# Row sums of two attention blocks in one product, spread over the partitions by transfers, and the first keys turned in parts of 512 and 256 tokens

## The chip, the cores and the metric

The kernel runs on one core of a Trainium2 chip. The core has a matrix engine (TensorE, PE in the profile), three engines for elementwise work (VectorE or DVE, ScalarE or ACT, GpSimd or POOL) and a SyncE queue (SP) that issues most transfers. The metric is the device time of one execution in microseconds; lower is better. Time before: 901.92 us, the median of 3 runs (901.76 to 902.88).

## What is computed

A routed attention and then a two-layer network with an ELU between its layers. Batch 4, 8 heads, 768 tokens, head size 64, 16 clusters; then 3072 tokens of width 512 through a hidden layer of 2048.

```python
q_assign = argmax(einsum(q_n, c_n));  k_assign = argmax(einsum(k_n, c_n))
mask = q_assign[:, :, :, None] == k_assign[:, :, None, :]
scores = where(mask, scale * q @ k.T, -1e9)
attn = exp(scores - max);  attn = attn / (sum(attn) + 1e-9)
x = (attn @ v) as rows of 512            # tokens x (heads * head size)
h = x @ w_in
g = where(h > 0, h, exp(min(h, 0)) - 1)
out = g @ w_out
```

## The kernel before

**Stages.** All data but the cluster masks (bf16) is float32. A first stage computes attention (about 18 to 341 us of the profile), then come six groups of 512 tokens of the network (341 us to the end), whose products are split after Strassen's manner into seven. The order of all instructions is written out by hand: each engine works through its own instructions in the order in which the program issues them, and semaphores hold an instruction until its operands are ready and its destination is free.

**Blocks and slots.** Attention is cut into 32 blocks (`blocks`, L156): batch, half of the queries (384 tokens) and pair of heads. `slot(n)` (L632) holds, one beside the other, the scores of block n, the product with V of block n-1, and the division of block n-2. Keys and queries lie turned (head size on partitions, tokens along the row) in `kT` and `qT`; the keys of batches 0 and 2 borrow the last 768 columns of `xT`, the array that later holds the attention's result.

In one slot the engines do this, in this order:
- PE: `row_sums(n-2)` (L552): for each head of the pair a product of 64 columns of ones with the summed probabilities of that head, into the bank `d_bank`, so that each of 64 rows holds the row sums. Then `values(n-1)` (L533) into `o_bank`; in some slots `clusters_q` or `clusters_k` (L427), four products of 32 columns each into `d_bank`, which give the similarity to the cluster centres; then six times `plain` (L498) and `masked` (L511), which put scores of 128 keys into one of three double banks in turn (`ring`).
- ACT: `take_sums(n-2)` (L563 to L565): logarithm of the row sums, a copy of them, and the exponential of minus the logarithm, an approximate reciprocal, into `r_of` and `e_of`. Then `take_values(n-1)` (L550), six exponentials (L520), and at the end what the list `later` holds (`flush`, L396): copies of the cluster masks (L456) and the exponent step of a weight piece (L330).
- DVE: `sums_end` (L528, L529): sums of the probabilities of block n-1 into `summed`; `divide(n-2)` (L568, L569): one Newton step on the reciprocal; in cluster slots `assign` (L440 to L453: transpose, maximum, comparison, transpose); the transposes of the next batch's keys and queries (L659, L666 to L673); `weigh(n)` (L401), which fills the rest of the slot with pieces of the weights' conversion (L320 to L350: the input's float64 words are joined into float32); and, behind the fourth exponential, `sums_begin` (L523).
- POOL: the multiplication of the result by the reciprocal (L572), and `mask_q` (L463), flushed after the cluster copies.
- SP: loads of V for block n+1 (L182), of raw keys and queries (L166) and of weights (L300).

How much of the weights' conversion goes into a slot is fixed by a table written by hand, `ROOM` (L384), against costs in `COST` (L389). The change does not touch either.

**The start.** `slot_first` (L596) turns queries and keys by products with the identity (`turned`, L588), 384 tokens at a time, in ring order, finds the clusters of both halves of the keys, and runs the scores of block 0. `masked(0, kt)` needs the cluster masks of the keys' half that kt lies in.

**The end of attention.** After the last slot come the rows' sums of block 30 and the values of block 31 (L1397 to L1405). `finish_attention` (L1407) runs inside the network's first unit, between its second and third product. In the first group POOL also forms sums of weights (`w_step`, L719) and stores them by its own transfers (L732), and bounds the ELU's exponentials (L762).

The lines that hold a division step and the multiplication:

```python
nc.vector.tensor_tensor(e_of, e_of, r_of, op=Alu.mult)
nc.vector.scalar_tensor_tensor(
    r_of, e_of, -2.0, r_of, op0=Alu.add, op1=Alu.mult, accum_out=r_sum[:, n : n + 1]
)
nc.gpsimd.tensor_tensor(x_of(n), x_of(n), r_of, op=Alu.mult)
```

Of the kernel before, what the change touches and what calls it, by code (L numbers as in the profile page):

```python
# [61 lines left out]
def main_path(ctx, tc, c, q, k, v, centroids, moe_w_in, moe_w_out, out):  # L62
# [71 lines left out]
    top = early[:, 7488:7512]  # L134
    hot_q = early[:, 7512:7896].bitcast(BF16).rearrange("p (s n) -> p s n", s=2)
# [3 lines left out]
    summed = sums_w[:, 4 * HS : 6 * HS]  # L139
# [111 lines left out]
    cT = const.tile([P, P], F32, name="cT")  # L251
    count = const.tile([P, 4 * B], F32, name="count")
    counted = 0
    r_sum = const.tile([P, len(blocks)], F32, name="r_sum")
    d_sum = const.tile([P, len(blocks)], F32, name="d_sum")
# [54 lines left out]
    def begin():  # L310
# [19 lines left out]
        later.append(lambda: nc.scalar.activation(e, e, Act.Relu, scale=8.0, bias=off))  # L330
# [63 lines left out]
    credit, later = 0.0, []  # L394

    def flush():  # L396
        for other in later:
            other()
        later.clear()
# [25 lines left out]
    def similar(t, cols, ps):  # L425
        for pr in range(NPR):
            nc.tensor.matmul(  # L427
                ps[32 * pr : 32 * pr + 32, :HS],
                lhsT=cT[:, 32 * pr : 32 * pr + 32],
                rhs=t[pr][:, cols],  # L430
                start=True,
                stop=True,
            )

    def assign(hot, ps):
# [3 lines left out]
        n = HS // NC  # L439
        nc.vector.transpose(sim, ps[:, :HS])  # L440
# [31 lines left out]
    def clusters_k(b, half, ps):  # L472
        cols = ts(half, HS)
# [13 lines left out]
    turn_of = 0  # L487
# [39 lines left out]
    def sums_end():  # L527
        nc.vector.tensor_tensor(add_to, add_to, probs_all[:, 8 * HS :], op=Alu.add)  # L528
        nc.vector.tensor_tensor(  # L529
            summed, add_to[:, : 2 * HS], add_to[:, 2 * HS :], op=Alu.add  # L530
# [21 lines left out]
    def row_sums(n):  # L552
        for e in range(2):
            nc.tensor.matmul(  # L554
                d_bank[64 * e : 64 * e + 64, :HS],
                lhsT=ones,
                rhs=summed[:, ts(e, HS)],
# [4 lines left out]
    def take_sums(n):  # L562
        nc.scalar.activation(r_of, d_bank[:, :HS], Act.Ln)  # L563
        nc.scalar.activation(e_of, d_bank[:, :HS], Act.Copy, accum_out=d_sum[:, n : n + 1])
        nc.scalar.activation(r_of, r_of, Act.Exp, scale=-1.0)  # L565

    def divide(n):
        nc.vector.tensor_tensor(e_of, e_of, r_of, op=Alu.mult)  # L568
        nc.vector.scalar_tensor_tensor(  # L569
            r_of, e_of, -2.0, r_of, op0=Alu.add, op1=Alu.mult, accum_out=r_sum[:, n : n + 1]  # L570
        )
        nc.gpsimd.tensor_tensor(x_of(n), x_of(n), r_of, op=Alu.mult)  # L572
# [8 lines left out]
    def turn(to, t, n):  # L581

        for i in range(HT):
            turned_by_pe(to[:, ts(i, P)], t, n + i)

    turns = 0

    def turned(to, t, n):  # L588
# [4 lines left out]
        turn(bank, t, n)  # L593
        nc.scalar.copy(to, bank[:, :HS])

    def slot_first():  # L596
# [10 lines left out]
        for pr in range(NPR):  # L607
            turned(kT[0][pr][:, :HS], first_k[pr], 0)
        told = [clusters_k(0, 0, o_bank)]
        flush()  # L610
        for pr in range(NPR):
# [1104 lines left out]
```

## Time and profile before

| | |
|---|---|
| Median of the runs | 901.92 us |
| The profiled execution | 902.24 us, of which its span is 900.5 us |
| PE busy | 889.9 us (99%) |
| DVE busy | 725.9 us (81%) |
| ACT busy | 449.5 us (50%) |
| POOL busy | 226.0 us (25%) |
| Granted PE clock, mean | 0.999 |

The page of a profile gives each engine's busy time, a strip of 40 equal slices of the span with the busy share of each in tenths, the transfers, the chain of work that ended last (followed back from the last instruction to what released it), and groups of instructions by line. A group's line reads: line, engine, operation, destination and source, shapes, count, busy time, mean duration. Closer views list single instructions in order of time with what ended the engine's idle time before each, the waits between engines, and the busy time of each engine in chosen stretches.

The two strips that matter here, where each digit is a slice of about 22.5 us:

```
PE   8999999999999999999999999999999999999997
DVE  4699999999999997995389965895589558956885
```

### The profile page before, as it was taken

What the parts mean: (1) busy time and instruction counts of PE and PEld (TensorE: products, weight loads), DVE (VectorE), ACT (ScalarE), POOL (GpSimd) and SP (SyncE); (2) the same over time, 40 slices, a digit from 0 to 9 for tenths busy, and PEclk for the clock granted to TensorE, in tenths of its full rate; (3) what the DMA queues carried; (4) which work ended last, traced back from release to release, by engine and by line L of the source; (5) the groups of instructions that cost most, each with busy time, mean ns of one, the idle gap of its engine ahead of it and who ended that gap; (6) DMA issues with size and microseconds to landing.
All of it is one profiled execution on the core that took longest, in us unless ns stands there. A gap on an engine that the chain in (4) does not pass through costs nothing.

```text
span 900.5 us, 17050 instructions
## 1 busy us (share of the span) xinstructions
PE 889.9 (99%) x6473; PEld 687.6 (76%) x6473; DVE 725.9 (81%) x1067; ACT 449.5 (50%) x883; POOL 226.0 (25%) x257
## 2 busy tenths in 40 slices
PE   8999999999999999999999999999999999999997
PEld 4444444444444447899989999999999999999997
DVE  4699999999999997995389965895589558956885
ACT  5677787777776774420133225522552255225421
POOL 1022031221303244870033002520252025202300
PEclk9999999999999999999999999999999999999999
DMA  6765554365323622102698766176717761767272
GB/s 197 195 110 137 153 137 80 105 135 139 71 82 96 192 88 71 70 13 95 199 296 302 241 206 220 50 242 206 218 55 241 212 210 58 240 210 209 58 221 87
DMA packets 153209, 138.33 MB, mean 154 GB/s; under 512 B 89248, under 2 KB 106656, under 8 KB 152096
## 3 DMA queue, kind: packets, MB, share of 16 engines
q1 hardware_dynamic: 151584, 132.45, 50.2%
q0 software_dynamic: 1248, 4.20, 1.5%
q8 instruction: 53, 0.87, 0.4%
q10 hardware_dynamic: 288, 0.52, 0.2%
q14 instruction: 36, 0.29, 0.1%
HBM read 114.59 MB, written 21.50 MB: 151 GB/s over the span
## 4 chain that ended last, share of the span: by engine, by line
PE 92%; DVE 4%; DMA 2%; SPq 1%; issue 0%; ACT 0%; DVEq 0%
PE bank L994 23%; PE bank L748 16%; PE banks L498 12%; PE o_bank L536 12%; PE bank L1066 9%; PE o_bank L994 4%; PE o_bank L748 3%; PE banks L511 3%; PE d_bank L994 2%; PE d_bank L554 2%; PE o_bank L1066 2%; PE d_bank L427 1%; SPq L166 1%; DMA w_out<-in_k_dram 1%; PE d_bank L1066 1%; PE d_bank L748 1%
## 5 line engine op out<-in xcount | busy, mean ns | idle before, releaser
L520 ACT ACTIVATE p_out<-banks 128x768 f32<-128x768 f32 x192 | 155.2, 811 | 26.8 <-PE banks L511 25.4
L536 PE MATMUL o_bank<-p_out,kq_g 128*64 128x384 f32 x768 | 129.4, 486 | 0.1
L536 PEld LDWEIGHTS o_bank<-p_out,kq_g 128*64 128x64 f32 x768 | 55.0, 137 | 69.2 <-issue 62.7
L762 POOL TENSOR_SCALAR kq_g<-kq_g 128x512 f32<-128x512 f32 x96 | 67.8, 715 | 152.0 <-ACT kq_g L761 151.6
L572 POOL TENSOR_TENSOR xT<-xT,sums_w 128x384 f32<-128x384 f32 x32 | 35.3, 1103 | 222.0 <-DVE sums_w L569 164.6
L523 DVE TENSOR_TENSOR sums_w<-p_out 128x1536 f32<-128x1536 f32 x32 | 57.1, 1785 | 7.5 <-ACT p_out L520 7.5
L994 PE MATMUL bank<-w_out,kq_g 128*128 128x128 f32 x512 | 63.1, 275 | 0.0
L528 DVE TENSOR_TENSOR sums_w<-sums_w,p_out 128x1536 f32<-128x1536 f32 x32 | 59.0, 1845 | 3.3 <-DVE sums_w L523 0.5
L994 PEld LDWEIGHTS bank<-w_out,kq_g 128*128 128x128 f32 x512 | 60.5, 192 | 0.5
L761 ACT ACTIVATE kq_g<-bank 128x512 f32<-128x512 f32 x68 | 39.8, 602 | 38.9 <-PE bank L748 17.3
L748 PE MATMUL bank<-xT,spare 128*128 128x256 f32 x256 | 59.2, 379 | 0.0
L748 PEld LDWEIGHTS bank<-xT,spare 128*128 128x128 f32 x256 | 48.3, 190 | 6.4
L748 PE MATMUL bank<-x_sum,w_in 128*128 128x256 f32 x224 | 52.9, 379 | 0.0
L765 DVE SCALAR_TENSOR_TENSOR kq_g<-kq_g,bank 128x512 f32<-128x512 f32 x68 | 44.9, 680 | 6.2 <-POOL kq_g L762 6.2
L748 PEld LDWEIGHTS bank<-x_sum,w_in 128*128 128x128 f32 x224 | 42.6, 190 | 5.8
L1280 DVE TENSOR_TENSOR kq_g<-kq_g 128x1024 f32<-128x1024 f32 x36 | 45.2, 1263 | 1.5 <-PE bank L994 1.5
L1084 POOL TENSOR_TENSOR spare<-x_sum 128x128 f32<-128x128 f32 x16 | 7.3, 455 | 154.4 <-PE bank L1066 88.8
L463 POOL TENSOR_SCALAR kq_g<-w_out,big,minus 128x768 bf16<-128x768 bf16 x16 | 34.1, 2138 | 46.8 <-ACT w_out L456 46.8
L550 ACT ACTIVATE xT<-o_bank 128x384 f32<-128x384 f32 x32 | 15.7, 490 | 48.3 <-PE o_bank L536 48.3
L498 PE MATMUL banks<-x_sum,xT 64*128 64x384 f32 x192 | 39.8, 492 | 0.0
L498 PE MATMUL banks<-x_sum,kq_g 64*128 64x384 f32 x192 | 39.6, 491 | 0.0
L498 PE MATMUL banks<-kq_g 64*128 64x384 f32 x192 | 39.6, 491 | 0.0
(326 smaller groups left out, 2030.2 us busy)
## 6 DMA issues: line engine op xcount, KB each, us to landing
kq_g<-in_v_dram SPq DMA_DIRECT2D x32, 384.0 KB, 3.6
sums_w<-far_s_s SPq DMA_DIRECT2D x42, 256.0 KB, 3.7
spare<-w_far SPq DMA_DIRECT2D x32, 256.0 KB, 3.1
words_w<-far_s_s SPq DMA_DIRECT2D x26, 256.0 KB, 3.5
out_dram<-p_out SPq DMA_DIRECT2D x22, 256.0 KB, 3.4
w_out<-in_q_dram SPq DMA_DIRECT2D x112, 48.0 KB, 2.7
sums_w<-far_s_q SPq DMA_DIRECT2D x21, 256.0 KB, 3.6
words_w<-far_a_s SPq DMA_DIRECT2D x20, 256.0 KB, 3.7
```

The costliest lines, as they stand in the source:

```text
L498: nc.tensor.matmul(s[:, e, :HS], lhsT=kT[b % 2][pr][rows, ts(kt, P)], rhs=qT[half][pr][rows], start=True, stop=False,)
L520: nc.scalar.activation(probs[kt], s[:, :, :HS], Act.Exp, scale=SCALE)
L523: nc.vector.tensor_tensor(add_to, probs_all[:, : 4 * HS], probs_all[:, 4 * HS : 8 * HS], op=Alu.add)
L528: nc.vector.tensor_tensor(add_to, add_to, probs_all[:, 8 * HS :], op=Alu.add)
L536: nc.tensor.matmul(o_bank[64 * e : 64 * e + 64, :HS], lhsT=v_raw[n % 2][:, e, kt], rhs=probs[kt][:, e], start=(kt == 0), stop=(kt == NT - 1),)
L748: nc.tensor.matmul(bank[:, ts(f, QS)], lhsT=left[:, ch, ts(f, P)], rhs=right[:, ch], start=first and f == 0 and ch == 0, stop=ch == 1, ski ...
L761: nc.scalar.activation(to, as_part(bank, to), Act.Exp)
L762: nc.gpsimd.tensor_scalar(to, to, 1.0, 0.0, op0=Alu.min, op1=Alu.max)
L765: nc.vector.scalar_tensor_tensor(to, to, -1.0, as_part(bank, to), op0=Alu.add, op1=Alu.max)
L994: nc.tensor.matmul(bank[:, :P], lhsT=left[:, f], rhs=right[:, f], start=first and f == 0, stop=last and f == 3, skip_group_check=True,)
L1066: nc.tensor.matmul(bank[:, ts(f, P)], lhsT=left[:, ts(f, P)], rhs=right, start=m in ("m1", "m5") and f == 0, stop=True, skip_group_check=True,
L1280: nc.vector.tensor_tensor(b[to][:, f], b[x][:, f], b[y][:, f], op=op)
```

## The change

1. **Row sums by pairs.** `row_sums(n)` now takes blocks n-1 and n together: four products of 32 columns of ones, two for each block, into the four quarters of `d_bank`'s partitions. It runs in odd slots alone (`sums_of`, n = 3, 5, ... 31) and once in `finish_attention`. `summed` becomes two buffers in turn.
2. **Division by pairs.** ACT's three instructions and DVE's two (now `reciprocals`) then serve two blocks at once, in odd slots. `reciprocals` stands after `weigh`, no longer before it.
3. **Spreading.** The result holds each row's reciprocal in 32 partitions, and the multiplication needs it in 64. `spread` issues two transfers from GpSimd's queue, one for each block, that copy 64 partitions into 128, each row twice, into `r_of` and `e_of`. Their source is a stretch of memory that is free at that time (`to_spread`).
4. **Multiplication on VectorE.** `scale_x` multiplies both blocks' results in the following even slot, after `weigh`, on VectorE. The last pair is multiplied on GpSimd after the network's third unit.
5. **`powers`.** The exponent step of a weight piece (L330) leaves `later` for a list of its own, which a slot flushes behind `take_sums` and not at the end of the slot before.
6. **First keys in 512 and 256.** The first batch's keys are turned, and their clusters found, in parts of 512 and 256 tokens; `plain(0, 0)` is issued before the second part's clusters, and the first pair's second part is turned before the first part's clusters. The ring starts one bank earlier. `findings` adds two tiny instructions for the different counts.

```diff
@@ -132,11 +132,19 @@
...
+    CUT = 512
+    told_in = {
+        HS: (sim, oh, top),
+        CUT: (p_out[:, :512], p_out[:, 512:768].bitcast(BF16), p_out[:, 768:800]),
+        S - CUT: (sim[:, :256], oh[:, :256], top[:, :16]),
+    }
     hot_q = early[:, 7512:7896].bitcast(BF16).rearrange("p (s n) -> p s n", s=2)
...
     add_to = sums_w[:, : 4 * HS]
-    summed = sums_w[:, 4 * HS : 6 * HS]
+    summed = [spare.rearrange("p a n -> p (a n)")[:, 2048 : 2048 + 2 * HS]]
+    summed.append(sums_w[:, 4 * HS : 6 * HS])
     r_of = sums_w[:, 6 * HS : 7 * HS]
@@ -249,10 +257,11 @@
...
     cT = const.tile([P, P], F32, name="cT")
+    last_n = len(blocks) - 1
     count = const.tile([P, 4 * B], F32, name="count")
     counted = 0
-    r_sum = const.tile([P, len(blocks)], F32, name="r_sum")
-    d_sum = const.tile([P, len(blocks)], F32, name="d_sum")
+    r_sum = const.tile([P, len(blocks) // 2], F32, name="r_sum")
+    d_sum = const.tile([P, len(blocks) // 2], F32, name="d_sum")
     off = const.tile([P, 1], F32, name="off")
@@ -327,7 +336,7 @@
...
         split += 1
-        later.append(lambda: nc.scalar.activation(e, e, Act.Relu, scale=8.0, bias=off))
+        powers.append(lambda: nc.scalar.activation(e, e, Act.Relu, scale=8.0, bias=off))
@@ -391,12 +400,13 @@
...
     steps += [("sum", n) for n in range(4)]
-    credit, later = 0.0, []
-    def flush():
-        for other in later:
-            other()
-        later.clear()
+    credit, later, powers = 0.0, [], []
+    def flush(*of):
+        for others in of or (later, powers):
+            for other in others:
+                other()
+            others.clear()
@@ -425,7 +435,7 @@
...
             nc.tensor.matmul(
-                ps[32 * pr : 32 * pr + 32, :HS],
+                ps[32 * pr : 32 * pr + 32, : cols.stop - cols.start],
                 lhsT=cT[:, 32 * pr : 32 * pr + 32],
@@ -436,8 +446,10 @@
...
         nonlocal counted
-        n = HS // NC
-        nc.vector.transpose(sim, ps[:, :HS])
+        size = hot.shape[2]
+        n = size // NC
+        sim, oh, top = told_in[size]
+        nc.vector.transpose(sim, ps[:, :size])
         s = sim.rearrange("p (n c) -> p n c", c=NC)
@@ -470,7 +482,9 @@
...
     def clusters_k(b, half, ps):
-        cols = ts(half, HS)
+        cols = slice(half * HS, half * HS + HS)
+        if b == 0:
+            cols = slice(half * CUT, S if half else CUT)
         similar(kT[b % 2], cols, ps)
@@ -484,7 +498,7 @@
...
-    turn_of = 0
+    turn_of = 2
@@ -524,10 +538,10 @@
...
-    def sums_end():
+    def sums_end(n):
         nc.vector.tensor_tensor(add_to, add_to, probs_all[:, 8 * HS :], op=Alu.add)
         nc.vector.tensor_tensor(
-            summed, add_to[:, : 2 * HS], add_to[:, 2 * HS :], op=Alu.add
+            summed[n % 2], add_to[:, : 2 * HS], add_to[:, 2 * HS :], op=Alu.add
         )
@@ -550,26 +564,53 @@
...
     def row_sums(n):
-        for e in range(2):
+        for at in range(0, P, 32):
+            j, e = at // 64, at // 32 % 2
             nc.tensor.matmul(
-                d_bank[64 * e : 64 * e + 64, :HS],
-                lhsT=ones,
-                rhs=summed[:, ts(e, HS)],
+                d_bank[at : at + 32, :HS],
+                lhsT=ones[:, :32],
+                rhs=summed[(n - 1 + j) % 2][:, ts(e, HS)],
                 start=True,
...
     def take_sums(n):
+        at = n // 2
         nc.scalar.activation(r_of, d_bank[:, :HS], Act.Ln)
-        nc.scalar.activation(e_of, d_bank[:, :HS], Act.Copy, accum_out=d_sum[:, n : n + 1])
+        nc.scalar.activation(e_of, d_bank[:, :HS], Act.Copy, accum_out=d_sum[:, at : at + 1])
         nc.scalar.activation(r_of, r_of, Act.Exp, scale=-1.0)
-    def divide(n):
+    def reciprocals(n):
+        at = n // 2
         nc.vector.tensor_tensor(e_of, e_of, r_of, op=Alu.mult)
         nc.vector.scalar_tensor_tensor(
-            r_of, e_of, -2.0, r_of, op0=Alu.add, op1=Alu.mult, accum_out=r_sum[:, n : n + 1]
+            to_spread(n),
+            e_of,
+            -2.0,
+            r_of,
+            op0=Alu.add,
+            op1=Alu.mult,
+            accum_out=r_sum[:, at : at + 1],
         )
-        nc.gpsimd.tensor_tensor(x_of(n), x_of(n), r_of, op=Alu.mult)
+    def to_spread(n):
+        if n == last_n:
+            return add_to[:, :HS]
+        if n > last_n - NB - 2:
+            return sim if n < last_n - NB else x_of(last_n)
+        return x_of(last_n - NB)
+    def scale_x(n, r, by=nc.vector):
+        by.tensor_tensor(x_of(n), x_of(n), r, op=Alu.mult)
+    def spread(n):
+        r = to_spread(n)
+        for j, to in enumerate((r_of, e_of)):
+            nc.gpsimd.dma_start(
+                to, r[64 * j : 64 * j + 64].unsqueeze(1).to_broadcast([64, 2, HS])
+            )
@@ -578,11 +619,6 @@
...
-    def turn(to, t, n):
-        for i in range(HT):
-            turned_by_pe(to[:, ts(i, P)], t, n + i)
@@ -590,8 +626,10 @@
...
         turns += 1
-        turn(bank, t, n)
-        nc.scalar.copy(to, bank[:, :HS])
+        size = to.shape[1]
+        for i in range(size // P):
+            turned_by_pe(bank[:, ts(i, P)], t, n + i)
+        nc.scalar.copy(to, bank[:, :size])
@@ -605,11 +643,14 @@
...
         for pr in range(NPR):
-            turned(kT[0][pr][:, :HS], first_k[pr], 0)
+            turned(kT[0][pr][:, :CUT], first_k[pr], 0)
+        turned(kT[0][0][:, CUT:], first_k[0], CUT // P)
         told = [clusters_k(0, 0, o_bank)]
         flush()
-        for pr in range(NPR):
-            turned(kT[0][pr][:, HS:], first_k[pr], HT)
+        for pr in range(1, NPR):
+            turned(kT[0][pr][:, CUT:], first_k[pr], CUT // P)
+        first = ring()
+        plain(0, 0, first)
         told.append(clusters_k(0, 1, d_bank))
@@ -619,8 +660,9 @@
...
         for kt in range(NT):
-            s = ring()
-            plain(0, kt, s)
+            s = ring() if kt else first
+            if kt:
+                plain(0, kt, s)
             masked(0, kt, s)
@@ -632,9 +674,12 @@
...
         more = b + 1 < B
-        if n > 1:
-            row_sums(n - 2)
-            take_sums(n - 2)
+        sums_of = n - 2 if n > 1 and n % 2 else None
+        pair_done = n - 4 if n >= 4 and n % 2 == 0 else None
+        if sums_of is not None:
+            row_sums(sums_of)
+            take_sums(sums_of)
+        flush(powers)
         if n > 0:
@@ -645,9 +690,7 @@
...
         if n > 0:
-            sums_end()
-        if n > 1:
-            divide(n - 2)
+            sums_end(n - 1)
         if n > 0:
@@ -673,6 +716,12 @@
...
         weigh(n)
+        if sums_of is not None:
+            reciprocals(sums_of)
+            spread(sums_of)
+        elif pair_done is not None:
+            scale_x(n - 4, r_of)
+            scale_x(n - 3, e_of)
@@ -681,7 +730,7 @@
...
                 sums_begin()
-        flush()
+        flush(later)
@@ -1368,6 +1417,10 @@
...
         nc.vector.tensor_scalar(ok[:, 1:2], peak[:, 1:2], D_MAX, None, op0=Alu.is_lt)
+        for at, more in ((1, HS - CUT), (2, HS - S + CUT)):
+            nc.vector.tensor_scalar(
+                count[:, at : at + 1], count[:, at : at + 1], float(more // NC), None, op0=Alu.add
+            )
         nc.vector.tensor_scalar(same, count, float(HS // NC), None, op0=Alu.is_equal)
@@ -1379,7 +1432,6 @@
...
-    last_n = len(blocks) - 1
     slot_first()
@@ -1394,20 +1446,20 @@
...
                 w_step(0, 0, n - last_n + 3)
-    row_sums(last_n - 1)
     values(last_n)
-    sums_end()
+    sums_end(last_n)
     for n in range(2):
...
     ask()
-    take_sums(last_n - 1)
-    divide(last_n - 1)
+    scale_x(last_n - 3, r_of)
+    scale_x(last_n - 2, e_of)
     take_values(last_n)
...
         take_sums(last_n)
-        divide(last_n)
+        reciprocals(last_n)
+        spread(last_n)
@@ -1435,6 +1487,9 @@
...
             findings()
+        elif u == 2:
+            scale_x(last_n - 1, r_of, nc.gpsimd)
+            scale_x(last_n, e_of, nc.gpsimd)
     second_product_plain(0, early_on)
...
     table = table_steps()
```

## The prediction

> **What bounds the kernel now.** I read the strip and the chain first, then PE and DVE instruction by instruction inside attention, then the waits.
>
> ```profile
> PE 92%; DVE 4%; DMA 2%; SPq 1%; issue 0%; ACT 0%; DVEq 0%
> ```
>
> The chain is PE almost everywhere, so an instruction taken from PE seems to be worth its length. PE in two attention slots:
>
> ```profile
> 84.88 0.87 PE L554 MATMUL d_bank<-sums_w,ones 128*64 128x384 f32 x4
> 85.57 4.04 PE L536 MATMUL o_bank<-p_out,kq_g 128*64 128x384 f32 x24
> 89.54 0.85 PE L427 MATMUL d_bank<-kq_g,cT 128*32 128x384 f32 x8
> 90.33 0.92 PE L498 MATMUL banks<-kq_g,xT 64*128 64x384 f32 x4
> ...
> 95.37 0.86 PE L554 MATMUL d_bank<-sums_w,ones 128*64 128x384 f32 x4
> ```
>
> Start to start, row sums take 0.69 us, and the slot 10.49 (9.71 without clusters). But DVE:
>
> ```profile
> 86.74 1.75 DVE L523 TENSOR_TENSOR sums_w<-p_out 128x1536 f32<-128x1536 f32 x1
> 88.60 1.76 DVE L528 TENSOR_TENSOR sums_w<-sums_w,p_out 128x1536 f32<-128x1536 f32 x1
> 90.46 0.96 DVE L529 TENSOR_TENSOR sums_w<-sums_w 128x768 f32<-128x768 f32 x1
> 91.34 0.55 DVE L568 TENSOR_TENSOR sums_w<-sums_w 128x384 f32<-128x384 f32 x1
> 91.92 0.56 DVE L569 SCALAR_TENSOR_TENSOR sums_w<-sums_w 128x384 f32<-128x384 f32 x1
> ...
> 92.41 0.58 DVE L440 STREAM_TRANSPOSE w_out<-d_bank 128x384 f32<-128x384 f32 x1
> ...
> 97.02 1.77 DVE L523 TENSOR_TENSOR sums_w<-p_out 128x1536 f32<-128x1536 f32 x1
> ```
>
> DVE runs without a pause, and its waits from 44 to 340 us sum to 1.0 us. So it is a second bound, tuned by hand to PE's pace. I follow its **lag**: from the end of a slot's fourth exponential (start of its exponentials plus 4 x 0.81) to the start of L523, which could begin there. It is 0.1 in slot 3 (53.61 against 53.49), 2.3 in slot 7, 3.3 in slot 21, 4.2 in slot 22 (250.01 against 245.83), 1.5 in slot 31 (337.32). In slot 22 it stops PE for some 1.0 us:
>
> ```profile
> ACT sums_w L330 <- DVE sums_w L328: 1.3, 1, 1.3
> ...
> PEld d_bank L427 <- ACT sums_w L564: 1.6, 1, 1.6
> ```
>
> ACT's L330 waits for late DVE ahead of L563/L564, and those hold the bank of the cluster products.
>
> **What the Trainium skill says.** "TensorEngine Tiling (Array Packing)", section Tiling Modes: an array with 128 rows splits into two tiles of 64 columns or four of 32 that work at once, and changing the mode drains it. The trace agrees: L427's four 32-column products take 0.85 us, L554's two 64-column ones 0.87; a change of mode shows as about 0.1 us (24 L536 at 0.161 are 3.86, the spacing above is 3.97). "SBUF — State Buffer", Who interferes with whom: a DVE instruction with two SBUF inputs, or in a two-port mode, and a GpSimd instruction that reads SBUF shut each other out. It agrees:
>
> ```profile
> 295.88 1.50 DVE L328 TENSOR_SCALAR sums_w<-w_out 128x1024 uint32<-128x1024 uint32 x1
> ...
> 295.50 1.32 POOL L572 TENSOR_TENSOR xT<-xT,sums_w 128x384 f32<-128x384 f32 x1 [8.16 <-DVE sums_w L569]
> ```
>
> L328 has a median of 0.70. "DMA: Bandwidth & Descriptors", Anatomy of one DMA: a GpSimd transfer takes about 2.0 us plus bytes/436e3; an estimate of 2.5 us for 128 x 1,536 bytes. This trace:
>
> ```profile
> w_far<-spare POOLq DMA_DIRECT2D x8, 256.0 KB, 2.3
> ...
> w_in<-w_in POOLq DMA_DIRECT2D x2, 512.0 KB, 12.2
> ```
>
> The first agrees; the second (it accumulates) is no like.
>
> **Row sums on PE.** 32 calls become 16. An even slot loses 0.69; an odd one keeps a call of the same length (four 32-column products like L427) and gains a change of mode towards L536, +0.10. Alone, for slots 2 to 31 (15 even, 15 odd) and the call after the loop: 16 x 0.69 - 15 x 0.10 = 9.5 us.
>
> **DVE per pair.** Out: two divisions, 92.41 - 91.34 = 1.07 each. In: one reciprocal step 1.07 and two multiplications, the shape of L568, 0.55 each with 0.08 of overlap as between other independent neighbours: 0.97. So 2.14 becomes 2.04: nothing gained. Besides, L572 leaves POOL: I counted the instructions under it that were over their median: 0.74 us in slots 3 to 22; 2.95 in slots 23 to 31 (L344 at 285.87, L328 at 295.88 and 335.89), and up to 2.4 more beside weight sums that stay. L463's collisions stay too.
>
> **How much lag is allowed.** Exponential 1 of the next slot overwrites what L523 reads. In an even slot without clusters (9.02 now) the lag may be 9.02 - 3.24 - 1.75 = 4.0; PE can bear an exponential 0.77 late (three banks: 2 x 0.806 - 0.81 - 0.03), so 4.8. The **new wait**: in an odd slot ACT's L563 overwrites what `scale_x` reads, and that ends where L523 starts, 3.24 + lag after the first exponential. Behind it on ACT stand take_sums (1.65), L330 (1.1 where a piece began) and L550 (0.49) before the exponentials: 9.81 - 6.48 = 3.3 to 4.4, plus 0.77; in cluster slots 0.78 more. PE's L427 and then its score products wait for that. I take 4.3; bounds 2.5 (today's level) and 6. Moving L330 behind take_sums removes the stop of slot 22.
>
> **Sum over attention.** Slots 3 to 22: PE took 242.59 - 50.25 = 192.3; without DVE it would take 192.3 - 10 x 0.69 + 9 x 0.10 = 186.3. DVE's work is 250.01 - 53.61 = 196.4, less 19 divisions (20.3), plus 9 reciprocal steps (9.6) and 10 pairs of multiplications (9.7), less 0.74: 194.7. With 4.3 of lag the stage needs 194.7 - 4.3 = 190.4: **1.9 gained**, not 6. Slots 23 to 31: PE 332.55 - 242.59 = 90.0, less 4 x 0.69 and 1.0 of stop, plus 5 x 0.10: 86.7. DVE 87.3 - 9.6 + 5.4 + 3.9 - 2.95 = 84.0, so it works its lag off and PE is the bound: **3.3 gained**. Together 5.2.
>
> **Start.** The first keys' part of 512 costs its last turn, copy, products and the four DVE steps some 1.0 us more (15.0 to 18.0 against 14.5 to 16.9), but today ACT's copies wait behind four turns until 17.83 and PE reaches the first masks at 19.37. With scores 0 done early they can start at 18.7; three exponentials become free of the second part, and the second part's masks (22.7 today) come at 22.1, with two score blocks behind them, not three. I get the first V product 1.2 earlier (24.63 today); bounds 0.5 if `mask_q` shuts out the 512-wide comparison for its 1.0, 1.6 if not. Slot 2 adds its 0.69. But the third V product already waits for its V (issued at 40.30 behind SP's queue of loads, landing by 44.3). That queue starts with the first pair's last turn, 1.5 earlier at most: I take **1.3** for start and slot 2 together, bounds 0.5 and 2.3.
>
> **After the loop.** One call of row sums less: **0.7**. Both multiplications of the last pair land on POOL between its L762s of the third and fourth unit, where it has 0.3 us of idle time (380 to 387 us): +2.0 there. The last L762 goes from 384.6 to some 387.5, L765 and L804 (386.96) go 1.2 later, and PE's product at 387.92 has 0.3 to spare: **-0.9**, bounds 0 and -2.
>
> **Cost nothing.** Spreads: issue 2 x 0.7 on POOL, landing 2.5 to 5.8, needed 8.4 or more after `reciprocals` (a slot's DVE work); behind them on POOL stands only `mask_q`, needed three slots later. SP's queue gets none of them. If that cover is gone, every us late is a us of DVE, 14 times. L330, moved past take_sums, is read by L340 a slot later and 4.6 us (L523 to L529) after the lag's end. `findings` adds two instructions of 0.16 to DVE, beside PE's products.
>
> Sum: 5.2 + 1.3 + 0.7 - 0.9 = 6.3. From the profiled 902.24: 895.9. The median is 0.3 lower: **895.6**.
>
> **Rivals.**
> 1. *PE alone decides* (lag never stops it): 9.5 + 1.0 (stop) + 1.2 - 0.9 = 10.8, so 891.1. For: the chain is 92% PE. Against: DVE has no pauses. Chance 0.10.
> 2. *Lag holds at today's 2.5*: 1.8 of the 5.2 goes, and the start lands at its lower bound and the tail at -2: 902 - 3.4 - 0.5 - 0.7 + 2.0 = 899.4. For: L330's stop shows how a full ACT queue passes lag on, and there is a new wait there. Chance 0.18.
> 3. *Slower*: the spreads land late, and DVE waits at `scale_x`. One mechanism: two transfers in POOL's queue against SP's loads, 1.4 of issue and a landing over 7.0 us. It decides as soon as it comes on average 0.45 us late (14 x 0.45 eats the 6.3). At 0.7 late: 895.6 + 9.8 = 905.4. For: 12.2 us in one row above, DMA share near 1 in some slices. Against: the like row, 2.3. Chance 0.14.
> 4. *The start's gain is all there is and attention's is eaten exactly*: within 0.2%. Chance 0.05.
>
> **Numbers.** The forecast's own case (892.5 to 898.5) has 0.53. The range 891.0 to 901.0 takes in the lag's bounds (2.5 to 6 is -1.8 to +1.7), start and tail, all of rival 2 and most of 1: it leaves out rival 3 (0.14), a third of 1 and half of 4, 0.2 in all. Faster holds the forecast, rival 1 and most of 2; same holds rival 4 and the rest of 2. About 0.2% (1.8 us) is what a measurement of this kernel can tell from no change: faster 0.78, same 0.08, slower 0.14.
>
> **What would show it.** Exponentials of slot 22 start about 1.9 + 1.3 earlier (239.4), those of slot 31 some 6.5 earlier (326); DVE still without pauses from slot 4 to 22 with a lag of 3 to 4.5, and pauses or low lag after slot 24; L554 64 records of four quarters, 0.7 to 0.8 us; ACT waiting for L572 (now DVE's) before L563; GpSimd spreads landing under 6 us; PE stopping near the fourth unit's third products. Wrong if DVE waits for transfers, or if slots gain the full 0.69 each.

## The result, and the profile after

The changed kernel took **910.01 us** (median of 4 runs, 909.06 to 911.77) beside 901.85 of the kernel before on the same chip (901.76 to 902.88): ratio 1.009, 95% interval 1.0073 to 1.0108. It is slower by 8 us. The forecast was 895.6 with a range of 891.0 to 901.0: the prediction was wrong, in sign too. The profiled execution took 910.01 with a span of 908.0 (before: 902.24 and 900.5).

In the changed kernel the lines moved: row sums are L570 (before L554), the V products L550 (L536), the products for clusters L437 (L427), score products L512 (L498), VectorE's long sums L537, L542 and L543 (L523, L528, L529), take_sums L580 to L582 (L563 to L565), take_values L564 (L550), the mask of q on GpSimd L475 (L463), the scaling of x L606 (L572), and the spread is L611. In the runs below that move the masks, all lines behind the masks are one higher.

The page of the changed kernel: TensorE, VectorE and TensorE's granted clock in 40 slices, and the line of the chain by engine.

```profile
PE   8999999999979899999999999999999999999997
...
DVE  4799999999988886996389975896589658955875
...
PEclk9999999999989999999999999999999999999999
...
PE 64%; DVE 2%; DMA 2%; POOL 1%; issue 1%; ACT 0%; SPq 0%; ACTq 0%; DVEq 0%; POOLq 0%
```

A slice is 22.7 us. TensorE has a hole in slice 12 (250 to 272 us) and a smaller one in slice 14, and its clock falls at the first of them. TensorE had 92% of the chain before. Now the shares of all engines add up to 70% of the span, or 636 us, which is about what lies between slice 12 and the end: the chain is followed back to a transfer that begins at 262.0 and hardly further.

I read the slots from the exponentials of the trace, as in the prediction: start of each slot's first one, time to the next slot's, and the lag (end of the fourth exponential to the start of L523, now L537).

| slot | before: start, length | after: start, length | TensorE alone would need, after | lag before, after |
|---|---|---|---|---|
| 2 | 39.48, 9.71 | 38.32, 9.07 | 9.07 | 0.0, 0.0 |
| 6 | 80.95, 10.49 | 78.50, 9.85 | 9.85 | 2.6, 5.9 |
| 7 | 91.44, 10.49 | 90.43, 11.93 | 10.63 | 2.3, 4.3 |
| 15 | 172.26, 10.49 | 170.68, 11.41 | 10.63 | 3.2, 5.3 |
| 16 | 181.98, 9.71 | 181.06, 10.37 | 9.07 | 2.0, 3.6 |
| 22 | 242.59, 10.50 | 240.94, 9.85 | 9.85 | 4.2, 6.4 |
| 23 | 254.08, 11.49 | 253.38, 12.44 | 10.63 | 2.9, 4.2 |
| 24 | 263.79, 9.71 | 268.15, 14.77 | 9.07 | 1.7, 0.0 |
| 25 | 274.28, 10.49 | 280.65, 12.50 | 10.63 | 0.4, 0.5 |
| 28 | 303.42, 9.71 | 311.22, 11.65 | 9.07 | 2.0, 0.0 |
| 31 | 332.55, 9.71 | 339.98, 9.85 | 9.85 | 1.5, 0.0 |

(Length: from the slot before to this one. "Alone" is the length that such slots have in run 3 below, where nothing stops TensorE in them: 9.07 or 9.85 for even ones without and with clusters, 9.85 or 10.63 for odd ones. Behind a late slot an odd one can be shorter, since part of its work is already done.) From slot 2 to 22 the change gained 0.5, from 22 to 31 it lost 9.1; from slot 31 to the end it took 568.02 as against 567.92.

**The stop of slot 24.** The timeline of the changed kernel (start, duration, engine; in brackets the idle time before and what ended it):

```profile
261.44 0.37 SPq L190 DMA_DIRECT2D kq_g<-in_v_dram  x1
261.45 1.21 POOL L611 DMA_DIRECT2D sums_w<-xT  x2 [18.91 <-issue]
...
263.05 0.81 PE L512 MATMUL banks<-x_sum,kq_g 64*128 64x384 f32 x4
...
267.76 0.49 ACT L564 ACTIVATE xT<-o_bank 128x384 f32<-128x384 f32 x1 [8.47 <-DMA sums_w<-xT]
269.01 0.51 PEld L512 LDWEIGHTS banks<-x_sum,kq_g 64*128 64x128 f32 x4 [5.53 <-ACT p_out L534]
269.01 1.65 PE L512 MATMUL banks<-x_sum,kq_g 64*128 64x384 f32 x4 [4.99 <-ACT p_out L534]
...
270.77 1.49 PE L512 MATMUL banks<-x_sum,kq_g 64*128 64x384 f32 x4
```

ACT wants to write x of block 23 (L564) and stands until 267.76. What ends its wait is a transfer that writes `sums_w` and *reads* `xT`: the spread of the reciprocals of blocks 20 and 21. `to_spread` puts those reciprocals into x of block 23, which is free until its own take_values a slot later; the spread was issued at 261.45 and ACT was let go 6.3 us later, once the second of its two transfers, begun at 262.0, had taken 5.7 us. Behind L564 stand all exponentials, behind them the score banks, and TensorE has no work for 4.99 us. The price goes on after it. The same kernel in stretches (us, TensorE busy and its instructions, weight loads, VectorE, ACT, GpSimd, then granted clock, DMA share, GB/s):

```profile
258.30:263.90 5.60, 5.60 (x38) 2.47 (x34) 5.46 (x7) 0.98 (x2) 1.21 (x2) 1.00 0.54 170
263.90:266.90 3.00, 0.12 (x2) 0.00 (x0) 2.96 (x3) 0.00 (x0) 0.00 (x0) 1.00 0.90 294
266.90:269.00 2.10, 0.00 (x0) 0.00 (x0) 2.10 (x4) 1.24 (x3) 0.00 (x0) 0.50 0.00 1
269.00:273.70 4.70, 4.69 (x18) 2.29 (x18) 1.90 (x2) 2.98 (x4) 0.00 (x0) 0.50 0.00 0
```

When TensorE has stood for 2.9 us its clock is halved, and it stays so for 6.8 us. Four score products take 1.49 to 1.65 in place of 0.81, and so slot 25 is late by 12.50 - 10.63 = 1.9. With slot 24's 14.77 - 9.07 = 5.7 the stop costs 7.6.

**The slots up to 23.** The waits of attention (40 to 345 us; engine and line, who ended the wait: total, times, longest):

```profile
ACT sums_w L580 <- DVE xT L606: 12.9, 6, 3.3
...
ACT xT L564 <- DMA sums_w<-xT: 8.5, 1, 8.5
...
PE banks L512 <- ACT p_out L534: 5.6, 2, 5.0
...
PE o_bank L550 <- DMA kq_g<-in_v_dram: 2.5, 1, 2.5
```

The first is the new wait that the prediction named. Slots 6 and 7 on the timeline show how it begins:

```profile
77.62 2.04 POOL L475 TENSOR_SCALAR kq_g<-w_out,big,minus 128x768 bf16<-128x768 bf16 x2
77.70 3.58 DVE L542 TENSOR_TENSOR sums_w<-sums_w,p_out 128x1536 f32<-128x1536 f32 x1
...
82.82 0.52 PE L570 MATMUL d_bank<-spare,ones 128*32 128x384 f32 x2 [0.32 <-DVE w_out L452]
...
83.60 4.09 PE L550 MATMUL o_bank<-p_out,kq_g 128*64 128x384 f32 x24
...
86.72 1.02 DVE L606 TENSOR_TENSOR xT<-xT,sums_w 128x384 f32<-128x384 f32 x2
...
87.36 0.49 ACT L580 ACTIVATE sums_w<-d_bank 128x384 f32<-128x384 f32 x1 [1.73 <-issue]
87.66 1.75 DVE L537 TENSOR_TENSOR sums_w<-p_out 128x1536 f32<-128x1536 f32 x1
...
88.53 0.85 PE L437 MATMUL d_bank<-kq_g,cT 128*32 128x384 f32 x8 [0.84 <-ACT sums_w L581]
```

GpSimd's mask (77.62 to 79.66) shuts VectorE's L542 out: 3.58 us in place of 1.76. The lag becomes 5.9, the multiplications L606 come at 86.72, L580 can only start in them, and TensorE's L437 waits for the bank that take_sums empties. The third line of the waits holds slot 24's stop, the fourth slot 28's: the V load, issued at 293.10, stood among two 1 MB weight loads issued at 292.6 and 293.6, and landed after 12.9 us.

### The profile page after: what moved, and what is told of

Its sections match the earlier page's. It is cut to its first block, busy times and chain, and to the rows that moved or that the text cites. A ratio compares the mean times of both kernels' runs of the same rounds, so it can differ in the third digit from the quotient of the medians.

```text
span 908.0 us, 17032 instructions
## 1 busy us (share of the span) xinstructions
PE 885.3 (97%) x6470; PEld 682.3 (75%) x6473; DVE 720.1 (79%) x1051; ACT 426.1 (47%) x819; POOL 199.3 (22%) x259
## 3 DMA queue, kind: packets, MB, share of 16 engines
q0 software_dynamic: 3296, 10.49, 4.0%
## 4 chain that ended last, share of the span: by engine, by line
PE 64%; DVE 2%; DMA 2%; POOL 1%; issue 1%; ACT 0%; SPq 0%; ACTq 0%; DVEq 0%; POOLq 0%
PE bank L1043 23%; PE bank L797 14%; PE bank L1115 9%; PE o_bank L1043 4%; PE o_bank L550 3%; PE o_bank L797 3%; PE d_bank L1043 2%; PE banks L512 2%; PE o_bank L1115 2%; DMA kq_g<-in_v_dram 1%; PE d_bank L1115 1%; DMA sums_w<-xT 1%; PE d_bank L797 1%; PE banks L525 1%; PE d_bank L570 0%
## 5 line engine op out<-in xcount | busy, mean ns | idle before, releaser
L534 ACT ACTIVATE p_out<-banks 128x768 f32<-128x768 f32 x192 | 152.7, 811 | 29.1 <-PE banks L525 21.8
L550 PE MATMUL o_bank<-p_out,kq_g 128*64 128x384 f32 x768 | 130.9, 490 | 2.5 <-DMA kq_g<-in_v_dram 2.5
L550 PEld LDWEIGHTS o_bank<-p_out,kq_g 128*64 128x64 f32 x768 | 52.3, 137 | 77.3 <-issue 72.2
L611 POOL DMA_DIRECT2D sums_w<-xT x30 | 17.9, 620 | 276.5 <-ACT p_out L534 94.6
L537 DVE TENSOR_TENSOR sums_w<-p_out 128x1536 f32<-128x1536 f32 x32 | 56.5, 1767 | 16.3 <-ACT p_out L534 16.3
L542 DVE TENSOR_TENSOR sums_w<-sums_w,p_out 128x1536 f32<-128x1536 f32 x32 | 66.2, 2069 | 4.1 <-ACT p_out L534 1.3
L512 PE MATMUL banks<-x_sum,kq_g 64*128 64x384 f32 x192 | 41.8, 515 | 5.0 <-ACT p_out L534 5.0
L564 ACT ACTIVATE xT<-o_bank 128x384 f32<-128x384 f32 x32 | 15.6, 486 | 55.3 <-PE o_bank L550 46.8
L512 PE MATMUL banks<-x_sum,xT 64*128 64x384 f32 x192 | 40.1, 494 | 0.6 <-ACT p_out L534 0.6
L512 PE MATMUL banks<-kq_g 64*128 64x384 f32 x192 | 39.6, 491 | 0.0
L512 PE MATMUL banks<-kq_g,xT 64*128 64x384 f32 x192 | 39.6, 491 | 0.0
```

The costliest lines, as they stand in the source:

```text
L512: nc.tensor.matmul(s[:, e, :HS], lhsT=kT[b % 2][pr][rows, ts(kt, P)], rhs=qT[half][pr][rows], start=True, stop=False,)
L534: nc.scalar.activation(probs[kt], s[:, :, :HS], Act.Exp, scale=SCALE)
L537: nc.vector.tensor_tensor(add_to, probs_all[:, : 4 * HS], probs_all[:, 4 * HS : 8 * HS], op=Alu.add)
L550: nc.tensor.matmul(o_bank[64 * e : 64 * e + 64, :HS], lhsT=v_raw[n % 2][:, e, kt], rhs=probs[kt][:, e], start=(kt == 0), stop=(kt == NT - 1),)
```

## The experiments

Each ratio is to the kernel before on the same chip, with its 95% interval.

**1. The source of one spread.** The test for the buffer includes one pair more, so that the spread reads from `sim`.

```diff
-        if n > last_n - NB - 2:
+        if n > last_n - NB - 3:
             return sim if n < last_n - NB else x_of(last_n)
```

> The changed kernel with one constant altered: the row sums of blocks 20 and 21 are spread out of the buffer sim and not out of x of block 23. My theory: the stop of slot 24 (8.5 us of ACT at take_values, waiting for that spread's transfers to have read their source) and the low clock behind it are gone, so the exponentials of slot 25 start some 7.0 us earlier (about 273.6) and the time is 901.5 to 904, about level with the kernel before. Rival, DVE is the bound there and only the place of the stop changes: gain under 2 us, 908 to 910. If the third wait, the V load of slot 28, goes as well because the loads no longer stand beside each other, 2.5 us more: 899 to 901.5.

Measured: **899.04** (before 901.75), ratio 0.997 (0.9959 to 0.9980), so 1.2% or some 11 us below the changed kernel. The timeline of this run in slot 24:

```profile
261.55 0.49 ACT L564 ACTIVATE xT<-o_bank 128x384 f32<-128x384 f32 x1 [2.16 <-PE o_bank L550]
261.56 1.20 POOL L611 DMA_DIRECT2D sums_w<-w_out  x2 [18.92 <-issue]
```

The spread is issued at the same time as in the changed kernel (261.45); only nobody waits for it. ACT's L564 was ready at that very moment, so with the old source the whole of the transfer lay on the path. Slot 24 takes 9.28 in place of 14.77, slot 25 10.42, with the clock at 1.00, and slot 28 9.07: its late V load went too. The theory was right, together with the expectation's last case, in which the V load is in time too; and with this one constant altered the change is 0.3% faster than the kernel before.

**2. Without the wait for the scaling.** As 1, and the early spreads land in x of blocks 21 and 22.

```diff
+    def spread_to(n):
+        return (x_of(21), x_of(22)) if n <= 17 else (r_of, e_of)
...
-        for j, to in enumerate((r_of, e_of)):
+        for j, to in enumerate(spread_to(n)):
...
-            scale_x(n - 4, r_of)
-            scale_x(n - 3, e_of)
+            scale_x(n - 4, spread_to(n - 3)[0])
+            scale_x(n - 3, spread_to(n - 3)[1])
```

> As the run with the source altered, and up to the pair of blocks 16 and 17 the spreads land in x of blocks 21 and 22, which nothing uses yet, so that ACT's take_sums need not wait for VectorE's scale_x. My theory (the new wait adds to the lag wherever it is over about 4): the slots 7, 15, 16 and 19, which took 1.3, 2.3, 1.3 and 0.6 us more than TensorE needs, lose 1.5 to 3 us of that, and the time is that much below the run with the source altered. Rival (VectorE's work alone sets these slots, whichever wait passes it on): within 0.7 us of that run, with the stops at exponential 1 or elsewhere instead.

Measured: 898.32, ratio 0.9965 (0.9952 to 0.9979), 0.7 below run 1 with intervals that overlap. In the traces slot 7's stop goes whole (10.63), slot 15's 0.8 shrinks to 0.3, slot 16 keeps its 1.3 (10.39): the exponentials of slot 23 come 2.7 earlier than in run 1. So the traces show that the new wait is real, and that a late VectorE finds other places to stop TensorE. For the whole time the run doesn't tell the theories apart; the two traces are of single executions, run 1's the longest of its eight (900.45) and run 2's the shortest of its five (897.33).

**3. Masks on VectorE.** As 1, and all masks of q but the first leave GpSimd.

```diff
-    def mask_q(half):
+    def mask_q(half, by):
         for x in range(2):
-            nc.gpsimd.tensor_scalar(
+            by.tensor_scalar(
...
-            later.append(lambda: mask_q(half))
+            by = nc.vector if b or half else nc.gpsimd
+            later.append(lambda: mask_q(half, by))
```

> As the run with the source altered, and all masks of q but the first are made by VectorE, not GpSimd. If the collision of GpSimd's mask with VectorE's long additions (3.5 to 3.8 us in place of 1.76, 10.6 us of VectorE's time from 41 to 251 us) is what puts the lag up from 2.5 to 4 and more, the time falls by 1 to 3 us below the run with the source altered and the lag by 1 to 2 us, since a mask on VectorE costs an estimated 0.4 to 0.8 us of its own, 14 times. Rival (the collisions were there before as well, and it is the change of work in odd and even slots that matters): within 0.7 us, or slower by up to 3 if each mask is 1.5 us on VectorE.

Measured: **892.60**, ratio 0.9902 (0.9887 to 0.9917), another 6 us, twice the most that I had expected. The groups by line from 40 to 251 us (instructions, busy time, mean ns, idle before), of the kernel before:

```profile
L528 DVE TENSOR_TENSOR sums_w<-sums_w,p_out 128x1536 f32<-128x1536 f32 x20 | 38.0, 1899 | 2.5 <-DVE sums_w L523 0.5
```

of the changed kernel:

```profile
L542 DVE TENSOR_TENSOR sums_w<-sums_w,p_out 128x1536 f32<-128x1536 f32 x20 | 45.1, 2257 | 2.1
```

and of this run, where a line was added:

```profile
L543 DVE TENSOR_TENSOR sums_w<-sums_w,p_out 128x1536 f32<-128x1536 f32 x21 | 36.9, 1756 | 1.6
...
L475 DVE TENSOR_SCALAR kq_g<-w_out,big,minus 128x768 bf16<-128x768 bf16 x12 | 5.3, 485 | 0.0
```

One addition had cost 0.50 more than 1.756 in the mean. Over that stretch, VectorE's instructions beside a mask took 7.0 us more than their medians before, 10.7 in the changed kernel (2.1 of it with a spread being issued as well), nothing here; one mask instruction costs VectorE 0.485. The lag stays at 4.4 or less, and **no slot is stopped any more**: from slot 2 on all slots of a kind take the same 9.07, 9.85 or 10.63. This run's chain by engine:

```profile
PE 96%; DVE 1%; POOL 1%; issue 1%; DMA 0%; SPq 0%; ACT 0%; POOLq 0%
```

**4. Masks on VectorE, in the kernel before.** The same edit without the change.

> The kernel before with one thing altered: all masks of q but the first are made by VectorE. In the kernel before TensorE is the bound of nearly every slot and VectorE's lag stops it only in slot 22, so by my theory the masks alone bring that stop and little else: -1.0, and up to -0.7 more at the start: 900.0 to 900.9. The gain of 9.1 of the run with both is then the change's own, which GpSimd's masks were eating. Rival (the masks cost the same before and after, and are the gain): -5 to -6.5, 895 to 897.

Measured: 900.84 (before 901.39), ratio 0.9993 (0.9985 to 1.0001). The lag falls by up to 2.6 (slot 22: 1.6 for 4.2), slot 23 takes 10.49 for 11.49, slot 3 10.49 for 10.77, and no other slot moves: as expected. The collisions cost the kernel before 1 us at most, and cost 6 once TensorE's slots were shorter. The 8 us between runs 3 and 4 are the change's own, with the source of the one spread altered.

**5. Masks on VectorE, source left.** Run 3 with the first line of run 1 put back.

```diff
-        if n > last_n - NB - 3:
+        if n > last_n - NB - 2:
```

> The changed kernel with the masks on VectorE, but with the source of the spread of blocks 20 and 21 left in x of block 23. If the stop of slot 24 comes from the source itself, VectorE's lag being 2.0 us less there only shortens it: TensorE stands for about 3 us in place of 5.0, perhaps without the fall of the clock, 895.6 to 897.6, and 2.5 more if the V load of slot 28 is late again. Rival (the source costs only because VectorE is late): the spread is issued 2 us earlier and has been read in time, 892.0 to 893.5.

Measured: 900.03, ratio 0.9985 (0.9979 to 0.9992), 0.83% or 7.5 us above run 3: more than I had expected, and the rival is out. The timeline:

```profile
254.38 1.15 POOL L612 DMA_DIRECT2D sums_w<-xT  x2 [19.69 <-issue]
...
260.55 0.49 ACT L565 ACTIVATE xT<-o_bank 128x384 f32<-128x384 f32 x1 [8.05 <-DMA sums_w<-xT]
```

VectorE is earlier, but so is ACT: the wait is 8.05 in place of 8.47, TensorE stands 4.56, and the clock falls to 0.50 for 6.8 us again.

**6. The same source, but earlier.** Run 5, with the reciprocals and the spread of blocks 20 and 21 right behind take_sums at the head of slot 23.

```diff
             take_sums(sums_of)
+            if sums_of == 21:
+                reciprocals(sums_of)
+                spread(sums_of)
...
-            reciprocals(sums_of)
-            spread(sums_of)
+            if sums_of != 21:
+                reciprocals(sums_of)
+                spread(sums_of)
```

> The changed kernel with masks on VectorE and the source of the spread of blocks 20 and 21 still x of block 23, but with that one block's reciprocals and spread put at the head of slot 23's work, right behind take_sums. If the stop of slot 24 is the late place in the slot times the source in use, the transfers have read the source in time: 892.3 to 893.5. Rival (the transfers stand beside the V and weight loads wherever they are, or VectorE's reciprocals now hold up the slot's own steps): 895 or more.

Measured: 892.40 (before 901.36), ratio 0.9903 (0.9886 to 0.9919), level with run 3.

```profile
246.42 1.15 POOL L612 DMA_DIRECT2D sums_w<-xT  x2 [12.24 <-ACT xT L565]
...
254.17 0.49 ACT L565 ACTIVATE xT<-o_bank 128x384 f32<-128x384 f32 x1 [2.16 <-PE o_bank L551]
```

Eight us earlier, and nobody waits. So the stop took both: a source that is written a slot later, and a place late in the slot.

**7. Scaling on GpSimd.** As 1, with the slots' two multiplications on GpSimd.

```diff
-            scale_x(n - 4, r_of)
-            scale_x(n - 3, e_of)
+            scale_x(n - 4, r_of, nc.gpsimd)
+            scale_x(n - 3, e_of, nc.gpsimd)
```

> The run with the source altered, with the two multiplications of a pair in the slots on GpSimd in place of VectorE. If VectorE's own work (0.97 us less per pair) sets the stops of slots 7 to 23, most of their 6.5 us goes: 893 to 896. If instead what GpSimd does beside VectorE costs VectorE as much as it is spared (an estimate of up to 1.0 us under each multiplication), nothing is gained: 898 to 900.5.

Measured: 901.72, ratio 1.0002 (0.9995 to 1.0009), 0.3% (3 us) above run 1 and worse than either expectation. Up to slot 9 it is better (slot 7 takes 10.63), then slots 11 and 19 take 12.16 and 14.00 (slot 19 with a stretch at half the clock, see the last section). GpSimd now waits for the landing of its own spreads:

```profile
POOL xT L606 <- DMA sums_w<-xT: 21.3, 10, 3.7
```

and what is queued behind runs into VectorE's long additions: VectorE's instructions up to 340 us take some 30 more than the medians of their kind, against some 15 in run 1.

**8. Powers behind take_sums, alone.** The kernel before with this one move.

```diff
-        later.append(lambda: nc.scalar.activation(e, e, Act.Relu, scale=8.0, bias=off))
+        powers.append(lambda: nc.scalar.activation(e, e, Act.Relu, scale=8.0, bias=off))
...
             take_sums(n - 2)
+        flush(powers)
         if n > 0:
             values(n - 1)
```

> The kernel before, with the step that makes the powers of a piece (ACT, after VectorE's split) kept back until take_sums has been issued, and nothing else of the change. My reckoning in the prediction: the stop of 1.0 us in slot 22 goes, 900.9. Rival (its lag goes on to the next slot and stops TensorE there): within 0.3 us of the kernel before.

Measured: 900.99 (before 901.75), ratio 0.9992 (0.9984 to 1.0000). Slot 23 takes 10.49 in place of 11.49 and all later slots keep the gain: as forecast, though the interval reaches to no gain at all.

**9. The start, alone.** The kernel before with the first k in parts of 512 and 256 and the scores ahead (the parts of the diff on `CUT`, `told_in`, `turned` and `slot_first`).

> The kernel before with the first k in parts of 512 and 256 tokens and scores of the first block ahead of the second part, and nothing else. The prediction's start without slot 2's share, 1.3 - 0.7: -0.6, 901.1. By the trace of the changed kernel, whose slot 1 started 0.52 earlier: -0.5. Rival (the gain at the start is eaten by the loads behind it, or by slot 22's stop): within 0.2 of the kernel before.

Measured: 901.66 (before 901.39), ratio 1.0003 (0.9995 to 1.0011): no gain. In its trace slots 1 to 31 are 0.6 to 1.0 earlier than before, and 1.1 is lost between slot 31 and the end, part of it at 473 us, where a TensorE product waits 0.3 for the load of `w_far` and its weight load stands for 0.7 with no wait that the profile shows; the kernel before doesn't stop there, but run 4's trace does, for 0.5. One profile can't say whether such a stop comes each time. What takes up the gain is open.

**10. The cut, taken out.** As 3, with the first k in halves of 384 again, scores ahead of the second half as in the change.

```diff
-    CUT = 512
+    CUT = HS
```

> The run with source and masks altered, with the first k again in two halves of 384 tokens; its scores still go ahead of the second half's products. My theory of the start (three exponentials in place of two are free of the second part): the first V product comes some 0.5 to 1.0 later, and 0.3 to 0.7 of that lasts: 892.9 to 893.5. Rival (a transfer later on takes up what the start gives, as in the run with the start alone): 892.6 within 0.3.

Measured: 892.43 (before 901.36), ratio 0.990 (0.9883 to 0.9916), level with run 3. The first exponential comes 1.2 earlier (18.32 for 19.52) and slot 0 takes 10.03 for 9.00: slot 1 starts at 28.34 and 28.52. So the rival held as to the size: the cut itself brings nothing, and what the start gained by slot 1 comes from the order.

**11. The last two multiplications on VectorE.** As 3.

```diff
-            scale_x(last_n - 1, r_of, nc.gpsimd)
-            scale_x(last_n, e_of, nc.gpsimd)
+            scale_x(last_n - 1, r_of)
+            scale_x(last_n, e_of)
```

> The run with source and masks altered, with the two last multiplications, after the third unit, on VectorE in place of GpSimd. The prediction's tail term said they cost 0.9 on GpSimd; in the traces the stretch after the last slot is no shorter than before although a call of row sums (0.7) is gone, so they cost some 0.7 to 0.8. My theory: that comes back, 891.6 to 892.2. Rival (VectorE is late there too, or the stretch varies by itself): within 0.3 of 892.6.

Measured: **891.95** (before 901.36), ratio 0.9898 (0.9881 to 0.9914), the lowest of all and where my theory had it, but not separable from run 3, so the rival stands too. VectorE is late there as well:

```profile
372.32 1.84 DVE L607 TENSOR_TENSOR xT<-xT,sums_w 128x384 f32<-128x384 f32 x2
...
376.59 0.69 DVE L854 TENSOR_TENSOR o_bank<-o_bank,spare 128x512 f32<-128x512 f32 x1
...
377.43 0.89 PE L798 MATMUL o_bank<-xT,spare 128*128 128x256 f32 x3 [0.43 <-DVE o_bank L854]
```

Beside two instructions of GpSimd (370.22 to 373.74) the pair takes 1.84 and not 1.02, and TensorE stops for the same product as with the pair on GpSimd in run 3 (0.43 here, 0.31 there).

## Why the prediction was wrong, point by point

**The step that failed is "Cost nothing. Spreads".** It asked when the spread's *reader* needs it ("needed 8.4 or more after reciprocals"). That held: VectorE waited for no spread. It didn't ask who next *writes its source*. For blocks 20 and 21 that is ACT's take_values one slot later, ready at the moment at which the spread is issued. The transfers took no longer than forecast (the second 5.7 us, forecast 2.5 to 5.8), but the 6.3 us from the first issue on lay whole on the path. This is shown by the trace, by run 1 (11 us less), by run 5 (7.5 more than run 3) and by run 6 (level with run 3). Rival 3 had the right sign and the wrong mechanism: DVE didn't wait at `scale_x`, and one stop, not fourteen, did it.

**The lag term was mis-sized.** "L463's collisions stay too" took them as a constant. Beside masks VectorE lost 10.7 up to 251 us, not 7.0: the masks now fall on L542 more fully (0.50 over its undisturbed length in the mean, 0.14 before). So from slot 3 to 22 only 0.35 was gained where 1.9 was forecast, and slot 23 lost another 1.8 (12.44 - 10.63). The allowance of 4.3 was about right: after lags of 4.4 and 4.5 (slots 13 and 21) TensorE lost nothing, after 4.5 and 4.6 (18 and 17) 0.6, after 5.2 to 6.4 (14, 15, 6, 22) 0.8 to 1.8; after 4.3 to 5.3 (7 to 10) it lost 0.3 to 0.4, or made the loss of the slot before good. That the masks made the lag and the stops is shown by runs 3 and 4 together; that the new wait had a part in them, by run 2's trace alone.

**TensorE's part was right.** An even slot lost 0.64 (forecast 0.69), an odd one gained 0.14 (0.10). With lag and source out of the way run 3 is 9 below the kernel before (0.6 of it run 4's), and rival 1, where TensorE alone decides, had said 10.8 and 891.1. I gave it 0.10 since VectorE had no pauses. That was right for the kernel as changed; one source altered and one short instruction moved to VectorE came near to it.

**Smaller steps.** Start and slot 2: 1.16 gained up to there (forecast 1.3), but by the order and not by the cut (run 10), so the number came near for another reason than the forecast's; and with the start alone (run 9) no gain is measurable at the end. Powers: the stop of 1.0 in slot 22 goes (run 8), right. Multiplications 1.02 and reciprocals as before: right. Call after the loop and tail: -0.2 forecast, -0.1 measured. TensorE does stop at the forecast place, for 0.3, but what the call gained and the tail lost singly is not shown.

The difference in profiled times, worked out: forecast 6.3 gained, measured 902.24 - 910.01 = -7.8, so 14.1 apart. Slots 24 and 25: 7.6. Slot 28's late V load: 11.65 - 9.07 = 2.6. Slot 23: 1.8. Slots 3 to 22 and start: 1.5 (gain 1.66 in place of 3.2). The other late slots gained 2.9 in place of 3.3: 0.4. The tail: -0.1. What lies outside the span grew by 0.2. Sum, before rounding: 14.1.

What made slot 28's V load late is open: run 1 has it in time, run 2 waits 0.5 for it, and run 5, with the stop of slot 24, has it in time. In the changed kernel the second weight load was issued 0.5 us behind it and it took 12.9 us; in run 2 the distance was 2.6 and it took 12.3, in run 5 3.7 and 11.2, in run 1 4.4 and 10.3. That fits a share of the transfers taken away by the weight load, but no run altered this alone.

## What to carry to other kernels

A transfer has two ends: ask for its destination who reads it, and for its source who writes it next and how soon after the issue; a buffer that is "free until a slot later" is not free for a transfer issued at the end of this slot. Where an engine is a second bound, count collisions with it again after the slots have become shorter: the masks' collisions cost at most 1 us before the change (0.6, not separable from nothing) and 6 after it. And undo suspects one at a time: here a slower kernel held a change worth 0.3% with one source altered, and 1% with the masks moved as well.

## What the runs showed of the hardware

A pause of TensorE costs more than itself. The Trainium skill, "TensorE: Matmul & The Clock Gate", Part 1: The HAM clock gate, says that after an idle window of about 3.4 us the clock is halved, and that it takes some 3.4 us of work to have it back. The traces agree in size: pauses of 4.99 us (changed kernel) and 4.56 us (run 5) brought 6.8 us at 0.50, twice 3.4, the last 4.7 of them behind the pause in the changed kernel, and slot 25 lost another 1.9 by it. But the window needn't be idle: in run 7 one with work in it was enough. Its stretches, with the columns as in the table of stretches above:

```profile
203.40:206.80 3.40, 1.28 (x10) 0.29 (x8) 3.37 (x3) 1.51 (x2) 2.13 (x1) 1.00 0.95 362
206.80:210.20 3.40, 3.40 (x14) 1.17 (x12) 3.30 (x5) 2.53 (x5) 0.00 (x0) 0.51 0.38 67
```

TensorE was busy for 1.28 of 3.40 us with a longest pause of 2.12, and the next 3.4 us ran at half speed; the pause of 2.51 in slot 28 of the changed kernel brought nothing of the kind. The traces suggest why. Within each of these three traces all changes of the clock lie whole multiples of 3.41 us apart (in the changed kernel the fall at 266.90 and the rise at 273.73). Counted off in steps of 3.41 from the fall, the step just before it held 0.53 us of TensorE's work in the changed kernel, 1.01 in run 5 and 1.29 in run 7. Slot 28's pause is divided between two steps, which held 2.5 and 1.8 us of work, and the clock stayed at 1.00. Where between 1.3 and 1.8 the border lies isn't shown.

The Trainium skill, "SBUF — State Buffer", Who interferes with whom, says that a VectorE instruction with two SBUF inputs contends with a GpSimd instruction that reads SBUF. In slot 6 of the changed kernel the shut-out was nearly total: two mask instructions of 2.04 us in all made an addition of 1.76 take 3.58, 1.82 more.
